# Score units of batch 0's second 256 tokens in pairs, a new order of pieces and pacing, and three late output tiles in halves: a sliding-window attention with a gated feed-forward on one Trainium2 core

## The chip, the cores and the metric

One core of one Trainium2 chip. The time is device microseconds of one execution; lower is better. Inputs and output are float32 in DRAM; the matmuls work on bf16.

## The reference, cut to what matters

```python
# q, k, v: (4, 8, 768, 64); n_sink = 4, window = 128
scores = q @ k.T / sqrt(64)
keep   = (pos_k < 4) | ((pos_q - pos_k >= 0) & (pos_q - pos_k < 128))
a      = softmax(where(keep, scores, -1e9))
x      = (a @ v)  -> (3072 tokens, 512)
a, b   = x @ w1, x @ w2            # 512 -> 1024
out    = ((a * b) @ w3) @ w_out    # 1024 -> 1024 -> 512
```

## The kernel before, in words

**Tiles.** A query block of 128 tokens sees its own key block, the one before it, and the four sink keys. Heads go in pairs (`NP` = 4). For batch 0's first two thirds (`BLOCKS` = (0,0), (0,1)) a score unit is a query block with some head pairs (`block_scores`): eight matmuls of 64 rows each into one PSUM tile `sc`, one exponential on ScalarE (`ex`), one mask product on VectorE (`am`). For the rest a unit is a head pair with 256 tokens (`scores`). `block_values` or `values` multiplies by v (`av`) and divides by the row sum (`xn`); the sinks have their own small matmul (`sink_scores`, tile `sp`, 32-column weights).

**Transposes.** kT, qT (`kqT`) and x (`xT`) are transposed on TensorE (`transposes`, tile `tp`; `xt`) for the early part, and by DMA from SP's queue for `XPOSE` and `X_XPOSE`: k and q of batches 2 and 3, x of batches 1 to 3.

**Feed-forward.** `w3 @ w_out` is multiplied out once, on the core: w3 blocks are transposed (`fold_w3`, tile `tp` from `w_sb`) and multiplied by `wo_sb` (`fold_mm`, tiles `ph` for row blocks 0 to 3, `pw` for 4 to 7) into `w3o`. `gate` computes x @ w1 and x @ w2 by pieces of 128 columns and 256 or 384 tokens (`pg`), ScalarE copies the one, VectorE multiplies; `project` multiplies by `w3o` (`po`), ScalarE copies to `o_sb` (in `w_sb`), and SP sends the 128x512 tile out. The last tile, (3, 5), goes in three parts of 256, 128 and 128 columns, the middle part over VectorE, the last part out by ScalarE's queue.

**Loads.** Nine float32 pieces of w3 and w_out (512 KB each, list `raws`) come over SP's queue and are cast on ScalarE ("act"), VectorE ("dve") or half on each ("both"). Everything else comes over GpSimd's queue in the order of `order`, with the cast on the way; GpSimd starts when the fifth raw piece has landed (`hold` = 5, the copy to `spent` in line 201), and has at most eight transfers under way.

**The order.** A planner at build time (`plan`) holds tasks with priorities, costs and due times of loads (`landings`), and writes out the instructions of TensorE, ScalarE, VectorE and SP one by one; each engine then runs its list in order. What matters here: `nudge` shifts priorities of single tasks; `PACE` holds score units apart; `started` lists tasks that must have begun before; a score unit with `slots=2` starts only when both `sc` buffers are free, so that its partner can follow at once. Where the planner sees TensorE without work before 40 us it puts in matmuls on a zero tile (`keep_busy`, tile `pz`), as many as fit the gap by its own costs:

```python
keep_busy(int((gap - 0.25) / (0.22 if start > 9.0 else 0.43)))
```

At the end the program waits on SP for eight counters of the DMAs issued by SP and ScalarE, one after the other; DMAs take these counters in rotation.

Of the kernel before, what the change touches and what calls it, by code (L numbers as in the profile page):

```python
# [21 lines left out]
def kernel(  # L22
# [13 lines left out]
    nc = tc.nc  # L36
# [8 lines left out]
    P = 128  # L45
# [3 lines left out]
    DM = H * D  # L49
# [4 lines left out]
    XPOSE = ((2, 0), (2, 1), (2, 2), (3, 0), (3, 1), (3, 2))  # L54
    BLOCKS = ((0, 0), (0, 1))
    SINKS = (1,)
    X_XPOSE = ((1, 0), (1, 1), (1, 2), (2, 0), (2, 1), (2, 2), (3, 0), (3, 1), (3, 2))
    SPLIT = 6
    scale = 1.0 / float(D) ** 0.5

# [66 lines left out]
    def load(what, *i):  # L127
# [9 lines left out]
        else:  # L137
# [1 line left out]
                load_w(dst, src, i[0] * 256, i[1] * 256)  # L139


    raws = [("wo", 2, 4, "act"), ("w3", 4, 5, "act"), ("w3", 0, 1, "both"), ("wo", 0, 2, "dve"),
            ("w3", 1, 2, "dve"), ("wo", 4, 6, "dve"), ("wo", 6, 8, "dve"), ("w3", 2, 3, "both"),
            ("w3", 3, 4, "act")]
    hold = 5

    order = [("w3", 5, 6), ("qkv", 0, 0, 1), ("qkv", 0, 1, 2), ("w3", 6, 8), ("qkv", 0, 2, 3),
             ("qkv", 0, 3, 4), ("w12", 0, 1), ("w12", 1, 2), ("w12", 2, 3), ("w12", 3, 4), ("qkv", 0, 4, 5),
             ("qkv", 0, 5, 6), ("qkv", 1, 0, 6), ("qkv", 2, 0, 6), ("qkv", 3, 0, 6)]

    nudge = {("g", 0, 2, 6, 0): -300, ("g", 1, 2, 4, 0): -1200, ("g", 0, 1, 3, 1): 60, ("fm", 6, 3): 1500}

    def flat(tile_, names):
        return tile_[:].rearrange(f"p {names} -> p ({names})")
# [42 lines left out]
    for h in range(H):  # L197
        r0 = 32 * (h // 2) + 4 * (h % 2)
# [246 lines left out]
    def project(b, m, n0, n1):  # L445

        po = ps_mm.tile([P, n1 - n0], FP32, tag="mm", name="po")
        for kk in range(KFF):
            nc.tensor.matmul(po[:], ab[b][:, kk, m * P:(m + 1) * P], w3o[:, kk, n0:n1],  # L449
                             start=(kk == 0), stop=(kk == KFF - 1))  # L450
        yield
        o_sb = w3_sb[:, (b * NB + m) % KFF, 2 * n0:2 * n1].bitcast(FP32)
        (nc.vector.tensor_copy if n0 == DM // 2 else nc.scalar.copy)(o_sb, po[:])  # L453
        yield
        t0 = b * S + m * P
        (nc.scalar if n0 > DM // 2 else nc.sync).dma_start(out=out[t0:t0 + P, n0:n1], in_=o_sb)
        yield

    def keep_busy(n):
# [61 lines left out]
    def task(name, prio, gen, stages, after=(), loads=(), ring=None, started=(),  # L521
             half=False, slots=1, paced=False):
        tasks[name] = dict(name=name, prio=prio + nudge.get(name, 0.0), gen=gen, stages=stages, after=list(after),
                           loads=list(loads), ring=ring, started=list(started), half=half,
                           slots=slots, paced=paced)
# [15 lines left out]
    for i in range(KFF):  # L541
        for h in range(2):
# [4 lines left out]
                 [x for a, _ in needs for x in a], [x for _, a in needs for x in a],  # L547
                 started=[("t3", i, 0)] if i >= SPLIT and h else [folded(i - SPLIT)] if i >= SPLIT else [], ring="mm")
        for h, (j0, j1) in enumerate(FM[i]):
# [10 lines left out]
                 started=[("fm", i - 1, 0)] if i < 4 and not begin and h == 0 else [])  # L560
            if last and (i % 2 or i >= 4):
                tasks["fm", i, h]["frees"] = ("fm", i if i >= 4 else i - 1, 0)
    unit = []
    last_av = []
    for b in range(B):
        for t in range(NT):
            kbs = (2 * t, 2 * t + 1)
            qk = []
            war = [("av", b - 2, NP - 1, NT - 1)] if b >= 2 else []
            for kb in kbs:  # L570
                if (b, t) in XPOSE:
                    for n, src, dst in (("k", kN[b], kT[b]), ("q", qN[b], qT[b])):
                        qk.append(("td" + n, b, kb))
                        task(qk[-1], 1, transposes_dma(src, dst, kb), [("sp", 1.4), ("dma", 1.2)],
                             war, [(n, b, kb)])
                else:
                    qk.append(("tpk", b, kb))
                    task(qk[-1], 1, transposes(b, kb), [("pe", 0.45), ("dve", 0.65)],
                         war, [("k", b, kb), ("q", b, kb)], "mm")
            if t == 0:  # L580
                task(("sk", b), 0, sink_keys(b), [("dve", 0.2)], [("sc", b, 1, 0)])
                task(("sv", b), 2, sink_values(b), [("dve", 0.6)],
                     [("av", b - 1, 1, NT - 1)] if b else [], [("vc",)])
            else:
                if b not in SINKS:
                    task(("ss", b, t), -1, sink_scores(b, t, t + 1), [("pe", 0.12), ("act", 0.4)],
                         qk + [("sk", b)], ring="mm", started=[] if (b, t) in BLOCKS else [("sc", b, 1, t)])
                elif t == 1:
                    more = [(n, b, kb) for n in (("tdk", "tdq") if (b, 2) in XPOSE else ("tpk",)) for kb in (4, 5)]
                    task(("ss", b, 1), -1, sink_scores(b, 1, NT), [("pe", 0.225), ("act", 0.6)],  # L590
                         qk + more + [("sk", b)], ring="mm", started=[("sc", b, 1, 1)])
            if (b, t) in BLOCKS:
                parts = [(j, r0, r0 + 2, [2 * i + r0 // 2]) for i, j in enumerate(kbs) for r0 in (0, 2)]
                if t == 0:
                    parts = [(0, 0, NP, [0, 1])] + parts[2:]
                for u, (j, r0, r1, avs) in enumerate(parts):
                    task(("sc", b, u, t), 4, block_scores(b, j, r0, r1),
                         [("pe", 0.23), ("act", 1.05), ("dve", 0.7)],
                         [("tpk", b, kb) for kb in (j - 1, j) if kb >= 0], ring="sc", paced=True,
                         started=([unit[-1][0]] if unit else []) + (unit[-4][1] if len(unit) > 3 else []))  # L600
                    for a in avs:
                        task(("av", b, a, t), 3, block_values(b, j, 2 * (a % 2)),
                             [("pe", 0.125 if j == 0 else 0.245 if j == 1 else 0.36), ("dve", 0.55)],
                             [("sc", b, u, t)] + ([("ss", b, 1 if b in SINKS else t), ("sv", b)] if t else []),
                             [("v", b, j)], "mm", last_av)
                        last_av = [("av", b, a, t)]
                    unit.append((("sc", b, u, t), [("av", b, a, t) for a in avs]))
                    if avs[-1] % 2:
                        task(("xt", b, 2 * (j % 2), t), 2.5, block_x_transposes(b, j),
                             [("pe", 0.225), ("act", 0.6)],  # L610
                             [("av", b, avs[-1] - 1, t), ("av", b, avs[-1], t)], [], "mm")
                continue
            for r in range(NP):
                after = list(qk)
                if b >= 2 and t == 0:
                    after += [("g", b - 2, len(CHUNKS[b - 2]) - 1, dt, 1) for dt in range(KFF)]
                lead = r % 2 == 0
                task(("sc", b, r, t), 4 if lead else 0, scores(b, r, t),
                     [("pe", 0.17), ("act", 0.83), ("dve", 0.58)] if t == 0 else
                     [("pe", 0.225), ("act", 1.05), ("dve", 0.7)], after, ring="sc",  # L620
                     slots=2 if lead else 1, paced=lead,
                     started=([unit[-1][0]] if unit else []) + (unit[-3][1] if lead and len(unit) > 3 else []))
                task(("av", b, r, t), 3, values(b, r, t),
                     [("pe", 0.187 if t == 0 else 0.36), ("dve", 0.55)],
                     [("sc", b, r, t)] + ([("ss", b, 1 if b in SINKS else t), ("sv", b)] if t else []),
                     [("v", b, kb) for kb in kbs], "mm", last_av)
                last_av = [("av", b, r, t)]
                unit.append((("sc", b, r, t), last_av))
                if not lead and (b, t) not in X_XPOSE:
                    task(("xt", b, r - 1, t), 2.5, x_transposes(b, r - 1, t),  # L630
                         [("pe", 0.225), ("act", 0.6)],
                         [("av", b, r - 1, t), ("av", b, r, t)], [], "mm")
            if (b, t) in X_XPOSE:
                for i in range(2):
                    task(("xd", b, t, i), 1, x_transposes_dma(b, t, i), [("sp", 1.3), ("dma", 1.2)],
                         [("av", b, NP - 1, t)])
    gates = []
    for b in range(B):
        for c, (t0, t1) in enumerate(CHUNKS[b]):
            last_t = (t1 - 1) // 256  # L640
            us = 0.65 * (t1 - t0) / 384
            for dt in range(KFF):
# [4 lines left out]
                     [x for t in range(t0 // 256, last_t + 1)  # L647
                      for x in ([("xd", b, t, 0), ("xd", b, t, 1)] if (b, t) in X_XPOSE else
                                [("xt", b, 0, t), ("xt", b, NP - 2, t)])] + war, [("w1", n), ("w2", n)], "mm",
# [15 lines left out]
    MARGIN = {"av": 0.3}  # L665

    YIELD = {"g": 0.0, "av": 0.0, "sc": 0.4, "tdk": 1.5, "tdq": 1.5}
    PACE = [[0, 1.3, 0], [0, 0, 0], [6.2, 0, 0], [5.3, 0, 0]]
    TURN, SHAPE = 0.095, {"sc": 1, "ss": 2}
    START, WARM_UNTIL = 1.2, 40.0  # L670
    BACKLOG = 1.6
# [165 lines left out]
```

## Time and profile before

| | |
|---|---|
| median of 3 runs | 196.19 us (195.68 to 196.28) |
| the profiled execution | 196.08 us |
| its span, first to last instruction | 194.4 us |
| TensorE busy | 188.2 us (97%), 1830 matmuls |
| ScalarE, VectorE, GpSimd busy | 103.9, 114.4, 75.6 us |
| moved by DMA | 29.17 MB, mean 150 GB/s |

Times in the profile count from the first instruction. "busy" is the union of an engine's instructions; a matmul of 512 columns is recorded with 0.38 us but the next one starts 0.22 us later, so the start times tell the pace. A line number is that of the kernel before; the changed kernel's are 2 to 8 higher.

### The profile page before, as it was taken

Reading aid. Unit: us, or ns where it says so; the run is one execution under the profiler, and the core shown is the slowest. Engines: PE = TensorE matmul, PEld = TensorE weight load, DVE = VectorE, ACT = ScalarE, POOL = GpSimd, SP = SyncE. Lnnn points to the kernel's source line nnn. Section 1 sums busy time; section 2 is a strip of 40 time slices with the busy share of each in tenths; the row PEclk is TensorE's granted clock in tenths of the full one; section 3 lists DMA queues with packets and bytes.
Section 4 is the critical chain, followed back from the end, with each engine's and each line's share of the span. In section 5 each row is a group of like instructions: output and inputs, shape, how many; then the busy total and the mean of one; then the engine's idle time right before and its main releaser. Section 6 shows DMA issues by size and latency. Waiting matters only on the chain.

```text
span 194.4 us, 4625 instructions
## 1 busy us (share of the span) xinstructions
PE 188.2 (97%) x1830; PEld 123.7 (64%) x1830; DVE 114.4 (59%) x277; ACT 103.9 (53%) x177; POOL 75.6 (39%) x102
## 2 busy tenths in 40 slices
PE   7899799999999999999999999999999999999993
PEld 2346376998867786788788455556666666644443
DVE  5465588755699987967678036778886434410000
ACT  3515369743866876566574376567773333333232
POOL 5199967689999944433364330000000000000000
PEclk9999999999999999999999999999999999999999
DMA  5999999999999999999999999999320200014334
GB/s 209 414 380 159 184 165 197 193 158 154 156 152 192 198 146 125 154 157 187 118 154 142 142 157 220 211 217 120 78 56 2 55 0 0 0 55 164 146 133 153
DMA packets 107589, 29.17 MB, mean 150 GB/s; under 512 B 98608, under 2 KB 103088, under 8 KB 107568
## 3 DMA queue, kind: packets, MB, share of 16 engines
q0 software_dynamic: 79520, 12.33, 90.5%
q1 hardware_dynamic: 27904, 16.49, 40.1%
q8 instruction: 14, 0.23, 0.5%
q10 hardware_dynamic: 144, 0.07, 0.1%
q14 instruction: 7, 0.06, 0.1%
HBM read 29.39 MB, written 6.29 MB: 184 GB/s over the span
## 4 chain that ended last, share of the span: by engine, by line
PE 82%; DMA 11%; POOL 3%; SPq 2%; issue 0%; DVE 0%; ACT 0%; DVEq 0%
PE pg L388 39%; PE po L449 21%; PE av L348 6%; PE sc L258 5%; DMA kqT<-qN 4%; DMA ab<-in_moe_w_dram 4%; DMA qN<-in_q_dram 3%; PE tp L211 3%; PE pw L435 2%; PE av L311 1%; PE sc L279 1%; SPq L375 1%; PE ph L435 1%; SPq L163 1%; PE sp L240 1%; POOL qN L108 1%
## 5 line engine op out<-in xcount | busy, mean ns | idle before, releaser
L388 PE MATMUL pg<-xT,w_sb 128*128 128x256 bf16 (+1 forms) x640 | 91.0, 294 | 0.0
L388 PEld LDWEIGHTS <-w_sb 128*128 128x128 bf16 x640 | 59.5, 98 | 20.1 <-issue 1.1
L395 ACT COPY a_sb<-pg 128x256 f32<-128x256 f32 (+1 forms) x80 | 33.3, 416 | 37.0 <-PE pg L388 22.5
L392 DVE TENSOR_TENSOR ab<-a_sb,pg 128x256 bf16<-128x256 f32 (+1 forms) x80 | 37.7, 472 | 24.8 <-PE pg L388 22.8
L449 PE MATMUL po<-w3o,ab 128*128 128x512 bf16 (+2 forms) x208 | 43.0, 363 | 0.0
L263 ACT ACTIVATE ex<-sc 128x1024 bf16<-128x1024 f32 (+1 forms) x40 | 37.6, 962 | 6.5 <-PE sc L258 5.9
L449 PEld LDWEIGHTS <-ab 128*128 128x128 bf16 x208 | 19.3, 98 | 20.4 <-issue 0.2
L267 DVE TENSOR_TENSOR am<-ex,maskt 128x1024 bf16<-128x1024 bf16 (+1 forms) x40 | 25.3, 646 | 9.9 <-ACT ex L263 9.9
L453 ACT COPY w_sb<-po 128x512 f32<-128x512 f32 (+2 forms) x25 | 14.1, 566 | 25.9 <-PE po L449 25.8
L108 POOL DMA_DIRECT2D vN<-in_v_dram x24 | 21.6, 902 | 12.9 <-DMA kN<-in_k_dram 9.9
L108 POOL DMA_DIRECT2D qN<-in_q_dram x24 | 22.1, 919 | 9.9 <-DMA vN<-in_v_dram 6.2
L108 POOL DMA_DIRECT2D kN<-in_k_dram x24 | 22.0, 918 | 7.7 <-DMA qN<-in_q_dram 5.4
L355 DVE TENSOR_TENSOR xn<-av,rec 128x256 bf16<-128x256 f32 x40 | 17.0, 425 | 1.4
L348 PE MATMUL av<-vN,am 128*128 128x65 bf16 x296 | 16.7, 193 | 0.0
L348 PEld LDWEIGHTS <-am 128*128 128x128 bf16 x296 | 14.5, 97 | 1.8 <-DVE rec L352 0.2
L258 PE MATMUL sc<-kqT 64*128 64x128 bf16 (+1 forms) x216 | 11.8, 238 | 0.2 <-DMA kqT<-qN 0.2
L453 DVE COPY w_sb<-po 128x128 f32<-128x128 f32 x1 | 0.3, 292 | 19.7 <-ACT w_sb L453 19.7
L348 PE MATMUL av<-vs,es 128*128 128x130 bf16 x56 | 11.0, 220 | 0.0
L213 DVE COPY kqT<-tp 128x1024 bf16<-128x1024 bf16 x12 | 8.3, 689 | 4.6 <-PE tp L211 4.4
L352 DVE RECIPROCAL rec<-av 128x4 f32<-128x4 f32 x40 | 7.1, 178 | 5.9 <-PE av L348 5.5
L258 PEld LDWEIGHTS <-kqT 64*128 64x128 bf16 x216 | 7.0, 94 | 4.6 <-issue 4.0
L283 ACT ACTIVATE ex<-sc 128x1024 bf16<-128x1024 f32 x7 | 7.2, 1026 | 4.2 <-PE sc L279 4.2
(71 smaller groups left out, 140.5 us busy)
## 6 DMA issues: line engine op xcount, KB each, us to landing
out_dram<-w_sb SPq DMA_DIRECT2D x23, 256.0 KB
kN<-in_k_dram POOLq DMA_DIRECT2D x24, 128.0 KB, 8.4
qN<-in_q_dram POOLq DMA_DIRECT2D x24, 128.0 KB, 8.2
vN<-in_v_dram POOLq DMA_DIRECT2D x24, 128.0 KB, 8.0
w_sb<-in_moe_w_dram POOLq DMA_DIRECT2D x9, 256.0 KB, 8.3
ab<-in_moe_w_out_dram SPq DMA_DIRECT2D x3, 512.0 KB
ab<-in_moe_w_dram SPq DMA_DIRECT2D x3, 512.0 KB
kN<-in_moe_w_out_dram SPq DMA_DIRECT2D x1, 512.0 KB
```

The costliest lines, as they stand in the source:

```text
L108: nc.gpsimd.dma_start(out=dst, in_=rows(src, b, kb))
L213: nc.vector.tensor_copy(kqT[b][:, :, :, kb * P:(kb + 1) * P], tp[:])
L258: nc.tensor.matmul(sc[:, e, c:c + n], kT[b][hp, r, kb * P:(kb + 1) * P], qT[b][hp, r, qb * P:qb * P + n], start=True, stop=True)
L263: nc.scalar.activation(ex[:, :, c0:], sc[:, :, c0:], ACTF.Exp, scale=scale)
L267: nc.vector.tensor_mul(am[:, :, c0:], ex[:, :, c0:], mk)
L348: nc.tensor.matmul(o, lhs, rhs, start=(n == 0), stop=(n == len(todo) - 1), skip_group_check=True)
L355: nc.vector.tensor_mul(xns[b, t][:, :, r, :, :], av[:, :, :, 0:D], rec[:].to_broadcast([P, 2, 2, D]))
L388: nc.tensor.matmul(pg[:], w_sb[:, kk, dt * P:(dt + 1) * P], xT[b][:, kk, tk], start=(kk == 0), stop=(kk == NP - 1))
L392: nc.vector.tensor_mul(ab[b][:, dt, tk], gate_a.pop((b, c, dt))[:], pg[:])
L395: nc.scalar.copy(a_sb[:], pg[:])
L449: nc.tensor.matmul(po[:], ab[b][:, kk, m * P:(m + 1) * P], w3o[:, kk, n0:n1], start=(kk == 0), stop=(kk == KFF - 1))
L453: (nc.vector.tensor_copy if n0 == DM // 2 else nc.scalar.copy)(o_sb, po[:])
```

## The change

Four things are edited. (1) In `BLOCKS`, the units of query blocks 2 and 3 (`PAIRS`) go in pairs: the unit with the first two head pairs leads (both `sc` buffers free), the other follows with priority 0 and without pacing. (2) The list `raws` is put in another order with other engines for the casts; `nudge` and `PACE` get other values. (3) One nudge takes columns 256 to 384 of the last tile ahead of the other tiles of batch 3. (4) Tiles (3, 1), (3, 2) and (3, 3) are sent out in two DMAs of 256 columns each.

```diff
+    PAIRS = (2, 3)
...
+    HALVED = ((3, 1), (3, 2), (3, 3))
...
-    raws = [("wo", 2, 4, "act"), ("w3", 4, 5, "act"), ("w3", 0, 1, "both"), ("wo", 0, 2, "dve"),
-            ("w3", 1, 2, "dve"), ("wo", 4, 6, "dve"), ("wo", 6, 8, "dve"), ("w3", 2, 3, "both"),
-            ("w3", 3, 4, "act")]
+    raws = [("w3", 1, 2, "both"), ("wo", 0, 2, "act"), ("w3", 0, 1, "act"), ("w3", 2, 3, "both"),
+            ("wo", 2, 4, "act"), ("wo", 4, 6, "act"), ("wo", 6, 8, "dve"), ("w3", 3, 4, "both"),
+            ("w3", 4, 5, "dve")]
...
-    nudge = {("g", 0, 2, 6, 0): -300, ("g", 1, 2, 4, 0): -1200, ("g", 0, 1, 3, 1): 60, ("fm", 6, 3): 1500}
+    nudge = {("g", 0, 1, 3, 1): 60, ("g", 1, 1, 1, 1): 300, ("t3", 4, 0): 30, ("p", 3, 5, 256): -300}
...
-        (nc.scalar if n0 > DM // 2 else nc.sync).dma_start(out=out[t0:t0 + P, n0:n1], in_=o_sb)
+        step = DM // 2 if (b, m) in HALVED else n1 - n0
+        for c in range(n0, n1, step):
+            (nc.scalar if n0 > DM // 2 else nc.sync).dma_start(out=out[t0:t0 + P, c:c + step],
+                                                               in_=o_sb[:, c - n0:c - n0 + step])
...
-                    task(("sc", b, u, t), 4, block_scores(b, j, r0, r1),
+                    lead, more = j in PAIRS and r0 == 0, j in PAIRS and r0 > 0
+                    task(("sc", b, u, t), 0 if more else 4, block_scores(b, j, r0, r1),
                          [("pe", 0.23), ("act", 1.05), ("dve", 0.7)],
-                         [("tpk", b, kb) for kb in (j - 1, j) if kb >= 0], ring="sc", paced=True,
-                         started=([unit[-1][0]] if unit else []) + (unit[-4][1] if len(unit) > 3 else []))
+                         [("tpk", b, kb) for kb in (j - 1, j) if kb >= 0], ring="sc",
+                         slots=2 if lead else 1, paced=not more,
+                         started=([unit[-1][0]] if unit else [])
+                         + (unit[-3 if lead else -4][1] if len(unit) > 3 else []))
...
-    PACE = [[0, 1.3, 0], [0, 0, 0], [6.2, 0, 0], [5.3, 0, 0]]
+    PACE = [[0.7, 0, 0], [0, 0, 0], [0, 3, 5.9], [5.9, 0, 0]]
```

In the lists that come out, TensorE has the same 1812 matmuls of real work in another order, and 23 `pz` matmuls instead of 18 (8 at the start and 15 after the first eight w3 transposes; before 13, 2 and 3).

## The prediction

> **What bounds the kernel now.** I read the page first, then the chain of waits that ended last, then TensorE's timeline.
>
> ```profile
> PE 188.2 (97%) x1830; PEld 123.7 (64%) x1830; DVE 114.4 (59%) x277; ACT 103.9 (53%) x177; POOL 75.6 (39%) x102
> ...
> PE 82%; DMA 11%; POOL 3%; SPq 2%; issue 0%; DVE 0%; ACT 0%; DVEq 0%
> ```
>
> TensorE is busy nearly always; the other engines have 40% and more to spare. The chain (start, length, what) shows the one place where it is set by data:
>
> ```profile
> 15.42 6.64 DMA qN<-in_q_dram
> 22.06 0.05 issue
> 22.11 0.40 PE tp L211 x4
> ```
>
> TensorE's timeline (start, length, instructions, in brackets the idle time before) around it:
>
> ```profile
> 1.33 5.73 PE L463 MATMUL pz<-ksbd 128*128 128x512 bf16 x13 [1.33 <-DVE ksbd L172]
> 7.03 0.62 PE L405 MATMUL tp<-ident,w_sb 128*128 128x128 bf16 x8
> 7.48 0.59 PE L463 MATMUL pz<-ksbd 128*128 128x512 bf16 x2
> ...
> 9.71 0.59 PE L435 MATMUL pw<-wo_sb,kN 128*128 128x512 bf16 x2
> 10.14 0.59 PE L435 MATMUL ph<-wo_sb,w3t 128*128 128x512 bf16 x2
> ...
> 20.62 0.39 PE L211 MATMUL tp<-ident,kN 128*128 128x128 bf16 x4
> 22.11 0.40 PE L211 MATMUL tp<-ident,qN 128*128 128x128 bf16 x4 [1.10 <-DMA qN<-in_q_dram]
> ...
> 23.20 0.59 PE L435 MATMUL ph<-wo_sb,w3t 128*128 128x512 bf16 x2
> 23.73 0.40 PE L279 MATMUL sc<-kqT 64*128 64x128 bf16 x8
> 24.06 0.60 PE L435 MATMUL ph<-wo_sb,w3t 128*128 128x512 bf16 x2
> ```
>
> Three readings. A 512-column matmul takes 0.216 us (9.71 to 10.14 for two), but 0.43 in the first row (5.73 for 13, the last with its drain): until about 7 us the clock is half. A 128-column transpose takes 0.056 (7.03 to 7.48 for eight). And TensorE waits 1.10 us at 22.11 for the second q block, in spite of which it never idles again for long. So the end is: 22.11, plus the work that lies behind that transpose, plus waits and losses behind it, plus the tail. What happens ahead of 22.11 counts only when it uses up the 1.10 us.
>
> **The start (raws, nudges): nothing.** Counted in the two lists, the work from the first w3 transpose to that q transpose is the same: 48 w3 transposes, 38 matmuls of 512 columns, 12 transposes of k and q, one score unit. Only `pz` differs. ScalarE's timeline shows when the first pieces land:
>
> ```profile
> 4.67 1.04 ACT L415 CAST wo_sb<-ab 128x1024 bf16<-128x1024 f32 x1 [2.58 <-DMA ab<-in_moe_w_out_dram]
> 5.92 1.04 ACT L415 CAST w_sb<-ab 128x1024 bf16<-128x1024 f32 x1 [0.21 <-DMA ab<-in_moe_w_dram]
> 7.20 0.62 ACT L415 CAST w_sb<-ab 128x512 bf16<-128x512 f32 x1 [0.23 <-DMA ab<-in_moe_w_dram]
> ```
>
> Pieces are of one size and land 1.28 us apart (4.64, 5.9, 7.2, so 8.5, 9.7 and on), whatever is in them. The first is now w3 block 1, cast half and half: ready at 4.64 + 0.62 = 5.3. Eight `pz` from 1.33 end at 1.33 + 8 x 0.427 = 4.75; the first eight transposes go at 5.3 and, at half clock, end at 6.2. Then 15 `pz`: two at half clock to 7.05, thirteen at 0.216, to 9.85. (w3 block 0 is cast by 8.3 and block 2 by 9.1, both covered.) Left to the q transpose: 40 + 12 transposes (2.9), 38 matmuls (8.2), the score unit 0.43: 21.4. That is 0.65 ahead of 22.06, where before it was 1.2 ahead. The landing itself stays: GpSimd's list is the same, and waits for the fifth piece as before. Cost nothing; cover left 0.65 us.
>
> **Pairs: -0.31.** A change between 128-row, 64-row and 32-column weights costs: 23.20 to 23.73 is 0.53 where two matmuls take 0.43, so 0.10 to enter; eight score matmuls take 0.33 (23.73 to 24.06), about 0.22 of it streaming, so 0.10 to leave. In the list before there are 15 such changes up to the first `pg` (seven units, one `sp`, once side by side); in the list after 12. In the whole program it is 62 and 59. Three at 0.10: 0.31, all behind 22.11. What might take it back is the last piece of w2 (rows of that piece alone, then TensorE):
>
> ```profile
> L111 POOL DMA_DIRECT2D w_sb<-in_moe_w_dram x1: 747/747/747, 30.7 to 30.7; - x1
> ...
> DMA to landing us min/median/max: 10.1/10.1/10.1
> ```
> ```profile
> 40.00 3.22 PE L388 MATMUL pg<-xT,w_sb 128*128 128x256 bf16 x28
> ```
>
> It lands at 40.8. Its first user is the 13th of these 28, at 40.00 + 12 x 0.109 = 41.3; with 0.31 less it comes at 41.0, 0.15 after the landing. It just fits: no wait, but 0.2 at most if it lands later.
>
> **Middle (PACE, order): -0.11 and +0.28.** One more wait stands in the timeline and the chain:
>
> ```profile
> 94.94 0.23 PE L258 MATMUL sc<-kqT 64*128 64x128 bf16 x2
> 95.34 0.56 PE L258 MATMUL sc<-kqT 64*128 64x256 bf16 x10 [0.17 <-DMA kqT<-qN]
> ```
> ```profile
> 87.58 7.72 DMA kqT<-qN
> ```
>
> The second matmul should come 0.11 after 94.94 and comes at 95.34: 0.29 lost to a q transpose by DMA that lands 7.72 us after its issue. In the list after, 8 `po` matmuls (1.73) are ahead of this score unit and 12 `pg` (1.31) are behind it: TensorE comes 0.42 - 0.31 = 0.11 later. SP's list is the same up to this transfer; if it lands at the same time, the wait shrinks by 0.11. If SP's string of transposes, which follows TensorE, moves up by 0.31 too, all 0.29 go. I take -0.11, the sure part.
>
> Against it stands the gate on the last x of batch 2. In SP's timeline before, and in TensorE's:
>
> ```profile
> 122.07 1.06 SPq L456 DMA_DIRECT2D out_dram<-w_sb  x2
> 123.22 3.19 SPq L375 DMA_TRANSPOSE xT<-xn  x2
> 126.50 1.23 SPq L218 DMA_TRANSPOSE kqT<-kN  x1
> ```
> ```profile
> 134.62 0.62 PE L258 MATMUL sc<-kqT 64*128 64x128 bf16 x12
> 135.16 1.15 PE L388 MATMUL pg<-xT,w_sb 128*128 128x384 bf16 x6
> ```
> ```profile
> L108 POOL DMA_DIRECT2D kN<-in_k_dram x1: 873/873/873, 102.7 to 102.7; - x1
> ...
> DMA to landing us min/median/max: 20.0/20.0/20.0
> ```
>
> Before, the pair of x transposes goes at 123.22 and 125.1, lands by the 7.72 above near 132.9, and is first read at 135.16. In the list after, that k transpose of batch 3 is ahead of the pair; its load lands at 102.7 + 20.0 = 122.7, so it can't go sooner; an output tile follows, then the pair: 122.75 + 1.23 + 0.1 + 0.53 + 0.1 = 124.7, the second 1.3 (as 1.23 and a gap) to 1.9 later (as before), at 126.0 to 126.6, landing at 133.7 to 134.35. And it is wanted sooner: 12 score matmuls with their two changes (0.55) and one `av` group (0.36) now come behind the gate, so 135.16 - 0.91 - 0.31 - 0.11 = 133.83. Wait: none to 0.55, I take 0.28.
>
> **The tail: -0.15.**
>
> ```profile
> 170.56 20.77 PE po L449 x112
> 191.34 0.02 issue
> 191.36 0.27 ACT w_sb L453
> ```
> ```profile
> 191.66 0.37 ACTq L456 DMA_DIRECT2D out_dram<-w_sb  x1
> ```
> ```profile
> L832 SPq EVENT_SEMAPHORE  x11: 17/28/28, 191.8 to 194.3; - x11
> ```
>
> TensorE's last 112 matmuls are the same in sum; taking 128 columns of the last tile to the front moves nothing at the end, since the last part is again 128 columns copied in 0.27 and sent by ScalarE. The halves are sent while SP has 1.73 us per tile for two issues of some 0.35: hidden. But three more DMAs turn the rotation: the last DMA had the fifth of the eight counters, so SP still walked three when it landed; now it has the eighth. Three waits of 0.028 are 0.08 at least; eleven of them from 191.8 to 194.3 are 0.23 each, 0.7 at most; I take 0.15, near the low end, since much of the 2.5 us is the landing itself.
>
> **Sum.** Against the profiled execution (196.08, span 194.4, 1.7 around it): 0 - 0.31 - 0.11 + 0.28 - 0.15 = -0.29, so 195.8; it was 0.1 under the median of the runs, so by the median 195.9. I stay at 195.8. A measurement of this kernel tells about 0.3% (0.59 us) from no change: faster is under 195.6, slower over 196.8.
>
> **Rivals.**
>
> *The x transposes come late (slower).* SP stands idle until the k block has landed, then sends four things in a row. If the load lands 1 us later, or the transfers take 1 us longer, the gate opens at 135.2: wait 1.4, total -0.57 + 1.4 = +0.8, 196.9. It eats the whole gain when the landing passes 134.4, and is slower past 135.0. For it: loads of that stretch take 20 us to land. Against it: fewer transfers of SP are under way by then, since its list stood still. 0.18.
>
> *The clock comes late.* Before, twelve 0.43 us matmuls run back to back up to 6.9 and the transposes at 7.03 are at full speed. After, there is a hole from 4.75 to 5.3 and eight transposes instead. If the clock is granted only after all 15 `pz`, they end at 6.2 + 6.4 = 12.6, 2.75 later; 0.65 is covered, some 0.4 is taken out of the later waits: +1.7 on the forecast, 197.5. It starts to cost at a grant after 8.3 us. Nothing in this trace tells how full the stretch must be. The Trainium skill (TensorE: Matmul & The Clock Gate, Part 1 and Part 4) says that the clock is granted after a busy free-running window of some 3.4 us, and that transposes don't count as busy in the same way; by that, the grant would slip by one window, to 10.4, an estimate by which the time would be 196.4. No run here shows it yet. 0.12.
>
> *Nothing comes of it.* The 0.31 is given back at the w2 landing (0.15 of room) and the gate, and the walk is short: 196.1. 0.15.
>
> *More comes.* The gate doesn't wait and SP's string moves up: -0.31 - 0.29 - 0.2: 195.25. 0.10.
>
> **How the numbers follow.** Forecast 0.45 (195.4 to 196.1 by itself), rivals 0.18, 0.12, 0.15, 0.10. Faster: a third of the forecast (0.18), the last rival, and a little for a q block that lands sooner, 0.31. Slower: the late gate 0.15, the late clock 0.07: 0.22. The rest is 0.47. The range from 195.2 to 197.0 leaves out the clock's worst and the tails.
>
> **What would show it.** Right: `pz` x15 ending near 9.9; still a wait for qN at 22.1, of about 0.6; score units x16 twice between 28 and 34; first `pg` 0.3 sooner; a wait under 0.3 at the score unit near 95; a wait under 0.6 for xT near 133.8; TensorE's end near 191.1. Wrong: no wait at 22.1, `pz` rows at 0.43 past 8 us, a wait of over 1 us for xT, or new waits for w_sb near 41.

## The result, and the profile after

The changed kernel is slower: 197.89 us against 196.12 us (medians of 22 runs each), a ratio of 1.0097 with a 95% interval of 1.0071 to 1.0122. The forecast was 195.8, the range ended at 197.0. The profiled execution took 197.75 us with a span of 196.0, where before it was 196.08 and 194.4. (Ratios leave out runs that are over 1.5% above the fastest of the same kernel, and medians do not; below, kernels are compared by ratios to the kernel before.)

The chain of waits of the changed kernel (start, length, what):

```profile
30.25 10.23 DMA w_sb<-in_moe_w_dram
...
40.53 1.92 PE pg L390 x16
...
86.53 9.58 DMA kqT<-qN
...
96.94 2.29 PE pg L390 x20
...
127.89 7.92 DMA xT<-xn
...
135.95 0.81 PE pg L390 x4
```

Before, the chain left TensorE once after 22 us, for one transfer of 7.72 us. Now it does so three times. TensorE's timeline shows what the second and the third are worth (the first, for w2, costs 0.30 and is taken up with the start below):

```profile
21.19 0.39 PE L213 MATMUL tp<-ident,qN 128*128 128x128 bf16 x4
...
42.28 0.39 PE L213 MATMUL tp<-ident,kN 128*128 128x128 bf16 x4
...
94.65 0.23 PE L260 MATMUL sc<-kqT 64*128 64x128 bf16 x2
96.16 0.56 PE L260 MATMUL sc<-kqT 64*128 64x256 bf16 x10 [1.28 <-DMA kqT<-qN]
...
134.37 0.34 PE L350 MATMUL av<-vN,am 128*128 128x65 bf16 x6
135.95 0.81 PE L390 MATMUL pg<-xT,w_sb 128*128 128x384 bf16 x4 [1.24 <-DMA xT<-xn]
...
172.19 20.92 PE L451 MATMUL po<-w3o,ab 128*128 128x512 bf16 x110
```

Up to 42.28 the change is a gain. The same transposes started at 43.06 before:

```profile
43.06 0.39 PE L211 MATMUL tp<-ident,kN 128*128 128x128 bf16 x4
...
170.40 20.92 PE L449 MATMUL po<-w3o,ab 128*128 128x512 bf16 x112
```

So TensorE leads by 0.78. At the score unit near 95 the second matmul should come 0.11 after 94.65 and comes at 96.16: 1.40 lost, where before it was 0.29. At the first read of the last x of batch 2 the matmul should come 0.18 after 134.37 and comes at 135.95: again 1.40, where before nothing was lost. The tail gains: from TensorE's end (193.11, before 191.32) to the end of the span (196.03 and 194.35 in the trace) it is 2.92, before 3.03. The sum is -0.78 + 1.11 + 1.40 - 0.11 = 1.62 of the 1.68 by which the span grew.

**Why the q block lands late.** Its transpose was issued at 86.53, 1.05 sooner than before (87.58), and still landed 0.8 later. Both programs have nearly the same transfers ahead of it: up to its landing the DMA engines had moved 18.30 MB before (at 95.30) and 18.37 MB after (at 96.11). The answer lies in the data rate of the DMA engines, here in the stretch from 92 to 98 us (40 slices of 0.15 us, GB/s; then, from the same view, queue 8, which carries instructions). The kernel before:

```profile
GB/s 159 158 151 113 20 20 155 155 163 157 161 157 151 155 157 150 142 148 158 160 160 157 159 259 147 149 142 107 42 9 8 8 10 8 36 155 161 159 152 160
...
q8 instruction: 1, 0.02, 1.0%
```

The changed kernel:

```profile
GB/s 202 150 159 154 160 138 26 9 32 151 138 154 160 158 265 149 149 148 149 141 61 0 5 8 9 10 9 58 136 158 161 160 158 157 162 159 156 153 136 155
...
q8 instruction: 1, 0.02, 1.2%
```

Each row has one high spike (259 and 265): a piece of instructions that arrives between the data. About 1 us behind it begins a hole in which next to nothing is moved, 10 GB/s and less where it was 155. (The shorter hole near 93 in both rows lies about 0.9 behind a smaller piece, 8 KB on another instruction queue, q14, at 91.7 before and 92.05 after.) Before, the spike is in the slice from 95.45 and the hole reaches from 96.35 to 97.1; the q block had landed at 95.30. After, the spike is in the slice from 94.1 and the hole reaches from 95.15 to 96.05; the q block is still under way and lands as the hole ends (86.53 + 9.58 = 96.11). The same hole lay behind the landing and now lies ahead of it. The page counts these pieces:

```profile
q8 instruction: 14, 0.23, 0.5%
```

14 pieces in 0.23 MB are 16 KB each. In the kernel before, the five whose spikes stand between 73.8 and 119.75 were each followed by such a hole, 0.75 to 0.9 us long, that began 0.9 to 1.05 behind the spike. The pieces can be placed by TensorE's instructions (weight loads and matmuls counted in the trace up to each piece): the one near 95 starts after some 2,040 to 2,060 of them in both kernels, and the next about 250 on. The Trainium skill (Runtime: NRT & Kernel Launch, Terms) says that each engine's instruction memory is refilled in blocks of 16 KiB; the trace agrees with its 0.23 MB in 14. The time of the hole thus follows TensorE's count of instructions: 0.78 us of lead and five more `pz` matmuls (ten instructions, 0.55 us at the 18 per us of the `pg` rows, a weight load and a matmul every 0.109 us) both bring it forward, together by 1.33; the spike moved by 1.35. That the hole belongs to the piece is so far an argument; the second series below tests it.

### The profile page after: what moved, and what is told of

It reads as the page before. It is cut to its first block, busy times and chain, and to the rows that moved or that the text cites. A ratio compares the mean times of both kernels' runs of the same rounds, so it can differ in the third digit from the quotient of the medians.

```text
span 196.0 us, 4622 instructions
## 1 busy us (share of the span) xinstructions
PE 188.2 (96%) x1820; PEld 124.3 (63%) x1835; DVE 114.2 (58%) x276; ACT 105.9 (54%) x179; POOL 75.2 (38%) x102
## 4 chain that ended last, share of the span: by engine, by line
PE 66%; DMA 22%; POOL 6%; SPq 2%; issue 1%; DVE 1%; ACT 0%; DVEq 0%
PE pg L390 33%; PE po L451 20%; DMA w_sb<-in_moe_w_dram 9%; PE av L350 6%; DMA kqT<-qN 5%; PE sc L260 5%; DMA xT<-xn 4%; DMA ab<-in_moe_w_out_dram 4%; POOL w_sb L113 2%; PE tp L213 2%; SPq L377 1%; POOL vN L110 1%; POOL qN L110 1%; SPq L165 1%; POOL kN L110 1%
## 5 line engine op out<-in xcount | busy, mean ns | idle before, releaser
L110 POOL DMA_DIRECT2D qN<-in_q_dram x24 | 21.5, 895 | 12.3 <-DMA vN<-in_v_dram 9.5
L468 PE MATMUL pz<-ksbd 128*128 128x512 bf16 x23 | 7.7, 503 | 1.3 <-DVE ksbd L174 1.3
L437 PE MATMUL ph<-wo_sb,w3t 128*128 128x512 bf16 x31 | 7.9, 380 | 0.1
```

Source lines behind the costliest of these rows:

```text
L110: nc.gpsimd.dma_start(out=dst, in_=rows(src, b, kb))
```

## Experiments

**First series: what set the two waits?** Two theories stood: that landings are fixed by what is queued for full DMA engines (drain), or by SP's issues (issue).

The pairs alone, on the kernel before:

```diff
+    PAIRS = (2, 3)
...
+                         slots=2 if lead else 1, paced=not more,
```

> The kernel before with the pairs alone; the raw pieces, nudges, pacing and output of before, and SP's list is that of before. Two theories. Drain: from about 60 to 137 us the DMA engines are never empty in either profile, and the last transfer of that backlog lands at 137.2 before and 137.3 after; so a transfer lands when the bytes ahead of it are through, and a lead of TensorE is lost at the next transfer that it needs. Then TensorE is 0.3 to 0.4 us ahead up to 95, the transposed q block still lands at 95.3 to 96.1, the wait there grows from 0.17 to 0.5 to 1.3, and the time is that of before, 196.1 (195.9 to 196.6). Issue: a landing follows its issue by about 8 us, and SP's issues follow TensorE; then everything moves up, the wait stays at 0.2 and the time is 195.8.

Measured: 196.45 us, ratio 1.0009 (0.998 to 1.0038), the "same" that drain wanted. But the profile, one of the short executions (195.19 us), shows neither a wait nor the loss:

```profile
42.37 0.39 PE L213 MATMUL tp<-ident,kN 128*128 128x128 bf16 x4
...
94.26 0.79 PE L260 MATMUL sc<-kqT 64*128 64x128 bf16 x12
```

The lead at the transposes is 0.69, of which 0.33 is a q block that landed sooner (21.78 instead of 22.11) and 0.36 the pairs. Nine of the twelve times lie in two heaps, four from 195.0 to 195.9 and five from 196.4 to 196.9 (the other three are 198.95 and up). Neither theory has two heaps.

The PACE of before in the changed kernel:

```diff
-    PACE = [[0.7, 0, 0], [0, 0, 0], [0, 3, 5.9], [5.9, 0, 0]]
+    PACE = [[0, 1.3, 0], [0, 0, 0], [6.2, 0, 0], [5.3, 0, 0]]
```

> The changed kernel with the PACE of before (raws, pairs, nudges and halves stay). Counted in the lists, the work between the late score unit near 95 and the first read of the last x of batch 2 is 1.86 us more than in the changed kernel, and the pair of x transposes stands one output tile (256 KB) further forward on SP. Drain and issue alike: the wait near 95 stays near 1.3 us, the x pair lands at 134 to 135.5, before TensorE comes for it near 136, so the 1.24 us wait for xT goes, and some 0.9 of the work that filled in behind the gate comes ahead: 197.2 (TensorE's end near 192.6). If the pacing has no part in the loss: 197.9, with an xT wait of over 1 us.

Measured: 197.66 us, ratio 1.0071 (1.0038 to 1.0104). The interval overlaps the changed kernel's, so what the pacing is worth stays open; it is not most of the loss. The one profile is of the longest execution (200.18 us), so whether the wait for xT goes in an ordinary one was not seen.

Less to drain, in both kernels, which so leave out 448 of the 512 columns of batch 0's output:

```diff
-            ... dma_start(out=out[t0:t0 + P, c:c + step], ...
+            ... dma_start(out=out[t0:t0 + P, c:c + (step if b else 64)], ...
```

> The changed kernel, but of batch 0's six output tiles only the first 64 of 512 columns are sent: 6 x 224 KB less for the DMA engines, five of the six before 95 us, all instructions and waits of the lists as they were. Drain: the transposed q block near 95 and the x pair land 1.5 us or more sooner, both waits (1.28 and 1.24) go, and the time is about 195.2. Issue: landings stay where SP's list puts them (8 to 9 us behind the issue), the waits stay over 1 us, the time stays 197.6 to 197.9.

> The kernel before with the same relief (64 of 512 columns of batch 0's six output tiles). Drain: only the 0.17 us wait near 95 (0.29 lost) is there to win: 195.8, and the q block there lands before 94.5. Issue: unchanged, 196.1. Either way this is the measure for what the relief itself brings: the changed kernel should gain about 2.5 us by it and this one 0.3, if the two waits are the loss.

Measured: 195.25 us for the changed kernel, ratio 0.9954 (0.9915 to 0.9992); 195.57 us for the kernel before, 0.9989 (0.9956 to 1.0023). The relief of the changed kernel is what drain forecast, but only half by its reason. The changed kernel with the relief:

```profile
96.01 0.56 PE L260 MATMUL sc<-kqT 64*128 64x256 bf16 x10 [1.29 <-DMA kqT<-qN]
...
134.23 0.34 PE L350 MATMUL av<-vN,am 128*128 128x65 bf16 x6
134.41 0.81 PE L390 MATMUL pg<-xT,w_sb 128*128 128x384 bf16 x4
```

The wait for xT is gone, the one near 95 is not touched by a megabyte less ahead of it: 1.29, as 1.28 without relief. So something else held the q block: in this run too a hole, from 94.85 to 95.9, lies just ahead of the landing. In the kernel before with the relief the twelve score matmuls run through from 94.68, so its 0.29 there did go, as drain forecast; its time can't be told from no change.

**Second series: move the piece of instructions.** Small matmuls on the zero tile change TensorE's count and nothing else. 14 of them, at the start of the kernel before:

```diff
         for _ in range(n):
             nc.tensor.matmul(pz[:], idle[:, 0:P], idle[:, 0:512], start=True, stop=True)
+        for _ in range(14 if n == 13 else 0):
+            nc.tensor.matmul(pz[:, 0:64], idle[:, 0:P], idle[:, 0:64], start=True, stop=True)
```

> The kernel before with 14 more matmuls of 64 columns on the zero tile at the start: 28 more TensorE instructions (some 0.5 us, covered by the 1.10 us wait at 22.11), all lists otherwise as before. Fetch theory: TensorE's instructions come in pieces of 16 KB by DMA; some 0.6 us after each such piece all DMA engines stand for about 1.2 us. Before, the piece comes at 95.5, behind the landing of the transposed q block at 95.30; 28 instructions more bring it 1.5 us sooner, to 94.0, ahead of that landing: the block lands near 96.5, the wait at the score unit grows from 0.17 to about 1.3, and the time is 197.2. Chance theory (that landing scatters by itself) and drain theory (bytes in the queue): the padding does nothing, 196.1.

Measured: 197.32 us, ratio 1.0068 (1.0034 to 1.0102). Rate and timeline of this run:

```profile
GB/s 151 155 143 83 20 103 121 132 145 230 138 152 135 139 116 16 1 7 8 10 10 8 20 160 160 158 160 156 151 155 159 153 132 158 158 155 157 159 161 158
```
```profile
94.62 0.23 PE L258 MATMUL sc<-kqT 64*128 64x128 bf16 x2
96.57 0.56 PE L258 MATMUL sc<-kqT 64*128 64x256 bf16 x10 [1.72 <-DMA kqT<-qN]
```

The spike has moved from 95.45 to 93.35 and the start of the hole from 96.35 to 94.25, the q block lands at 96.5 as forecast, and 14 matmuls that compute nothing and lie in a covered wait cost 1.2 us at this landing, 90 us later.

The other way round, fewer `pz` in the changed kernel (the second group, 15, is cut to 7):

```diff
-        for _ in range(n):
+        for _ in range(7 if n == 15 else n):
```

> The changed kernel with 7 instead of 15 matmuls on the zero tile in the second group: 16 TensorE instructions fewer, lists otherwise the same. Fetch theory: the piece of instructions that came at 94.2, and stopped the DMA engines from 94.84 to 96.15, comes 0.9 us later, the q block lands first, near 94.9, and the wait of 1.28 shrinks to 0.2 or less; the wait for xT near 135 stays or grows, since the lead of TensorE comes to it: 197.2, or 196.7 if the x pair gains too. Chance and drain theories: the wait near 95 stays at 1.2 to 1.3 and the time at 197.9.

Measured: 196.12 us, ratio 0.9995 (0.9956 to 1.0035), 1% better than the changed kernel by the removal of 16 instructions. Rate and timeline:

```profile
GB/s 158 154 158 154 150 50 30 157 151 133 155 154 163 159 161 159 154 158 159 266 129 143 154 144 150 149 157 70 13 9 10 83 154 159 134 149 157 155 154 155
```
```profile
94.52 0.62 PE L260 MATMUL sc<-kqT 64*128 64x128 bf16 x12
...
132.78 0.34 PE L350 MATMUL av<-vN,am 128*128 128x65 bf16 x6
132.96 0.82 PE L390 MATMUL pg<-xT,w_sb 128*128 128x384 bf16 x4
```

The spike is at 94.85, the hole only from 96.2, and the twelve score matmuls run through from 94.52. I had not expected that the wait for xT goes with it. SP's timeline tells why, first the changed kernel, then this one:

```profile
102.40 0.34 SPq L460 DMA_DIRECT2D out_dram<-w_sb  x1
...
126.00 3.19 SPq L377 DMA_TRANSPOSE xT<-xn  x2
```
```profile
101.30 0.55 SPq L460 DMA_DIRECT2D out_dram<-w_sb  x1
...
122.78 3.02 SPq L377 DMA_TRANSPOSE xT<-xn  x2
```

The lists are the same. With TensorE 1.5 us late behind the score unit (96.16 for 94.52 + 0.11), the next output tile is 1.1 late (102.40 for 101.30), everything behind it on SP too, and by the x pair 1.1 has become 3.2; what made it grow is not shown. So the second wait follows in part from the first. The changed kernel also has a hole ahead of this landing (from 132 to 136 us, 40 slices of 0.1 us):

```profile
GB/s 64 50 55 78 86 116 123 120 108 104 109 96 123 114 106 27 95 19 8 12 9 23 13 8 10 10 10 10 8 21 266 187 195 261 289 137 167 294 289 289
```

From 133.7 to 135.0 next to nothing is moved, and the x block lands at 135.82 (127.89 + 7.92). A wait of 1.24 could come from these 1.3 us or from the late issue; no run here parts the two. With 7 `pz` the x block is read at 132.96, and the 10 GB/s there, from 133.2 to 133.9, lie behind it. And with the relief above the second wait goes while the first stays. The profiled execution took 194.76 us; the twelve times spread from 194.73 to 197.51, so in some of them something is still late, which no profile shows.

Was it the count, or the shorter start? 16 small matmuls behind the 7:

```diff
+        for _ in range(16 if n == 15 else 0):
+            nc.tensor.matmul(pz[:, 0:64], idle[:, 0:P], idle[:, 0:64], start=True, stop=True)
```

> The kernel of the run with 7 zero matmuls of 512 columns, and behind them 16 more of 64 columns: TensorE's work and its start stay as in that run (16 x 0.03 us lie in its 1.02 us wait at 8.27), but it has 32 instructions more. Fetch theory: the piece of instructions near 95 comes 1.5 to 1.8 us sooner, near 93.4, the DMA engines stand from 94, ahead of the landing of the q block, the wait at the score unit is 1 us or more again, and the wait for xT follows it: 197.3 to 197.9. If the shorter start was what helped (other timing of the first loads, or the clock), nothing changes: 196.1.

Measured: 198.62 us, ratio 1.0122 (1.008 to 1.0163), somewhat worse than forecast; the profile is of the shortest of its six executions (197.45) and has both waits again:

```profile
96.33 0.56 PE L260 MATMUL sc<-kqT 64*128 64x256 bf16 x10 [0.77 <-DMA kqT<-qN]
...
135.67 0.81 PE L390 MATMUL pg<-xT,w_sb 128*128 128x384 bf16 x4 [0.78 <-DMA xT<-xn]
```
```profile
GB/s 141 147 157 156 208 152 153 158 160 127 59 9 80 242 141 144 152 148 151 147 145 140 87 15 10 10 51 162 152 136 157 161 157 159 157 158 162 154 160 136
```

The spike is at 93.95, 0.9 sooner than with 7 `pz` alone, and the hole from 95.45 to 95.9 lies ahead of the landing (96.29) again. So the two waits come with the count, not with the shorter start. They are not all of the difference between the two profiled executions (197.45 and 194.76): 0.8 of it was lost ahead of 43 us, where the last piece of w2 landed at 41.17 instead of 40.35, and why is open. That lateness also explains the spike, forecast near 93.4: 32 instructions are 1.8 sooner, less 0.8, so 1.0.

**Third series: a kernel that keeps the gains.** The changed kernel with 7 `pz` and with the first four output tiles sent when the DMA engines are idle:

```diff
+    LATE, kept = (0, 1, 2, 3), []
...
+        late = b == 0 and m in LATE
+        o_sb = (wo_sb[:, 2 * LATE.index(m):2 * LATE.index(m) + 2, :]... if late else w3_sb[...]).bitcast(FP32)
...
+        if late:
+            kept.append((t0, o_sb))
...
+        if (b, t, i) == (3, 0, 1):
+            for t0, o_sb in kept:
+                nc.sync.dma_start(out=out[t0:t0 + P, :], in_=o_sb)
```

> The kernel of the run with 7 zero matmuls, and besides the first four output tiles are kept (in the room of wo_sb, which is read no more by then) and sent only when the DMA engines are idle, past 137 us: 1 MB less in the queue, nothing left out. Fetch and drain together: both waits go (the x pair lands 3 us or more sooner), so about 2.5 us off the changed kernel: 195.2 to 195.5. If only the fetch matters: 197.2 or as the run beside it. If neither: 197.9.

Measured: 195.20 us, ratio 0.9948 (0.9919 to 0.9978): faster than both kernels, and all twelve executions from 194.71 to 196.16. Its profile has no wait for data near 95 or 135.

The kernel before with pairs, halves and third column part, without its last five `pz`:

```diff
+    PAIRS = (2, 3)
+    HALVED = ((3, 1), (3, 2), (3, 3))
...
-        for _ in range(n):
+        for _ in range(n if n > 5 else 0):
```

> The kernel before with the pairs, with the third column part of the last tile and the halves of the change's tail, and without the last five zero matmuls (10 TensorE instructions fewer, so that the piece of instructions near 95 comes some 0.5 us later than in the run with the pairs alone, where it came 0.8 us behind the q block). Fetch theory: the landing at 95 is never behind the stop, so the 0.4 us of the pairs and the 0.15 to 0.2 us of the tail stay: 195.2, with few runs over 196. Issue or chance theories: as the run with the pairs alone, 196.2, with the same two heaps of times near 195.2 and 196.5.

Measured: 195.73 us, ratio 0.9958 (0.9927 to 0.9989): faster. Eight of the twelve executions lie in one heap, 194.69 to 195.97, and the verdict rests on them; the four others, from 197.68 up, are what "few runs over 196" did not foresee. The one profile is of one of these (197.68). In it TensorE waits 1.21 for a load of q at 44.53, and 0.65 for the q block at 97.09, ahead of its piece of instructions at 97.7; so the forecast that no landing there is late failed in it, and what lengthened these four stays open. With the late output tiles as well:

> The kernel before with the pairs, the halves and the third column part, without the last five zero matmuls, and with the first four output tiles kept until the DMA engines are idle (as in the run of the changed kernel with late outputs): before's order of the middle with all that was found to help. Fetch and drain: no wait near 95 or 135 in any run, 195.0, at or just below the 195.2 of the changed kernel with late outputs. If the order of the changed kernel's middle was itself worth something: 0.3 us or more above it.

Measured: 194.92 us, ratio 0.995 (0.992 to 0.998), twelve executions from 194.37 to 196.33. It can't be told from the changed kernel with the same help, so the order of the middle is worth nothing that shows here. Its profile has no wait near 95 or 135 either.

## Why the prediction was wrong, point by point

The terms were forecast as 0 (start), -0.31 (pairs), -0.11 and +0.28 (middle) and -0.15 (tail). Measured, the first two are -0.78 together, and the others +1.11, +1.40 and -0.11.

- **The start ("cost nothing; the landing stays").** Too cautious, since the landing did not stay. A wait of 0.6 for qN was forecast; the transposes ran at 21.19 without one, because GpSimd issued this load at 14.54 instead of 15.42 (its copy to `spent` alone took 0.19 instead of 0.71). What ends next is the last piece of w2: the chain goes from its landing at 40.48 to `pg` at 40.53,

```profile
39.80 2.65 PE L390 MATMUL pg<-xT,w_sb 128*128 128x256 bf16 x20
```

  and these 20 matmuls, 2.18 at 0.109 each, take 2.48 up to the transposes at 42.28: 0.30 lost, where 0.15 of room and no wait were forecast. 0.78 was left of this lead and the pairs.
- **The clock.** The rival did not happen, nor did its condition in full: the first piece was cast at 4.02, not 4.64, so the eight transposes came right behind the `pz`, at 4.72, without the hole from 4.75 to 5.3. The transposes alone did not hold the clock up:

```profile
4.72 1.06 PE L407 MATMUL tp<-ident,w_sb 128*128 128x128 bf16 x8
5.57 4.10 PE L468 MATMUL pz<-ksbd 128*128 128x512 bf16 x15
9.51 1.06 PE L407 MATMUL tp<-ident,w_sb 128*128 128x128 bf16 x16
```

  15 `pz` in 3.94 us (5.57 to 9.51) are, by 0.427 and 0.216 each, 3.3 at half and 11.7 at full clock: full from 7.0, as before. The estimate of 10.4 by the Trainium skill (TensorE: Matmul & The Clock Gate, Parts 1 and 4) is not borne out here, where the transposes came but no hole; the measurement decides.
- **Pairs, -0.31.** Right, as far as one execution each tells: 0.36 in the kernel with the pairs alone.
- **Middle, -0.11.** This is the step that failed. It rested on "if it lands at the same time", from one row of 7.72 us, and took the same order of transfers for the same landing. The transfer took 9.58, and the term was +1.11: 0.82 because the second score matmul came later (96.16 for 95.34) and 0.29 of TensorE's lead that was lost in the wait. The working left out the rate of the DMA engines around 95, where the hole just behind the landing stood in the trace of before, and what the five added `pz` do to anything but the start.
- **The gate, +0.28.** Right place, wrong reason, and 1.40: the size of this term failed too. The k block was not what held SP: in the changed kernel its load went at 103.4 and took 17.9,

```profile
L110 POOL DMA_DIRECT2D kN<-in_k_dram x1: 881/881/881, 103.4 to 103.4; - x1
...
DMA to landing us min/median/max: 17.9/17.9/17.9
```

  so it was there at 121.3, and its transpose went only at 124.03, because SP's list was late from the first wait. The pair went at 126.00 instead of 124.7. In the run with 16 instructions fewer the same list has the pair out at 122.78, sooner than my 124.7, and no wait. The rival "x transposes come late" got the sign, the place and even the wait of 1.4 (196.9), but by luck: it blamed the load or the transfers and had nothing for the wait near 95, from which the late issue came.
- **The tail, -0.15.** Right: 0.11, near the lower bound of 0.08. From ScalarE's issue of the last DMA to the end of SP's last waits

```profile
193.44 0.37 ACTq L460 DMA_DIRECT2D out_dram<-w_sb  x1
```
```profile
L840 SPq EVENT_SEMAPHORE  x11: 17/28/28, 193.5 to 196.0; - x11
```

  it is 2.59 us (193.44 to 196.03), where it was 2.69 (191.66 to 194.35). This holds in all profiles: 2.69 to 2.72 in the four kernels with the old tail, 2.58 to 2.61 in the eight with the new one.
- **The chances.** Slower had 0.22, most of it on the rival above. No rival had a q block near 95 that lands late; the range ended 0.9 below the median.

## What to carry to other kernels

Where the DMA engines are full, a transfer that lands just in time can be upset by little: look at the data rate around it, slice by slice, for holes that lie just behind, and ask what moves them. A lead that TensorE wins early is worth only what the next transfers let through, and a late step on an in-order queue can grow on its way (here from 1.1 to 3.2), so find the first wait before explaining the second. When a change adds or drops filler instructions, count them over the whole program and not only in the gap they fill.

## What the runs showed of the hardware that was not expected

A 16 KB piece of TensorE's instructions comes by DMA every 250 or so of its instructions (14 in the program), and with the DMA engines full a hole of 0.45 to 1.2 us, under 25 GB/s where it was 155, began 0.9 to 1.4 us behind the spike in the first four runs whose rates from 92 to 98 us stand above, and 1.5 behind it in the fifth. The count of TensorE's instructions decides which transfer this hits: 28 more cost 1.2 us, 16 fewer took 1% off the time. Not every piece does it. In the last kernel (pairs and late output tiles) the piece in this stretch, the spike of 265, has none behind it:

```profile
GB/s 40 10 5 9 78 150 158 158 160 156 155 154 138 158 153 145 155 156 160 163 149 161 265 140 141 140 144 138 146 145 146 149 154 149 155 154 155 157 149 156
```

What it is in such a piece that halts the others, and why not always, stays open.
